# Attention, a mixture of experts and a dense layer on one core: where the guard's checks stand, and the order of two experts' first rows

## The chip, the cores and the metric

The kernel runs on one core of one Trainium2 chip. The metric is the device time of one launch in microseconds (us), the median of several runs. Each engine works through its own queue in order: PE (TensorE) multiplies matrices into PSUM, DVE (VectorE) and ACT (ScalarE) work element by element and also read PSUM, POOL (GpSimd) works on SBUF, and SP (SyncE) only issues DMAs. Engines wait for each other by semaphores.

## The reference, cut to what matters

Everything is float32. A recurrent attention with a decaying state per head is followed by a mixture of eight experts, of which each token takes one, and by a dense layer.

```python
B, H, S, D = 4, 8, 768, 40
for t in range(S):                       # attention: one state (D x D) per batch and head
    y[t] = r[t] @ state
    Sa = state @ a[t]
    state = state * w[t] - outer(Sa, b[t]) + outer(v[t], k[t])
x = y, heads side by side                # 3072 tokens x 320
e = argmax(x @ w_gate); g = softmax(x @ w_gate)[e]
x = g * (relu(x @ w1[e]) @ w2[e])        # 8 experts, 320 -> 1024 -> 320
h = x @ w_in                             # dense, 320 -> 2048 -> 320
out = (max(h, 0) + alpha * min(h, 0)) @ w_out
```

## The kernel before, in words

**Attention (class `Attention`).** The recurrence is solved in chunks of 64 steps. Four chunks of two batches make a group (`o`); there are six groups, and each needs per chunk and head the inverse of a triangular 64x64 matrix, called T here. `prepare` (L438) loads w, k, b and a and makes running products with two scans on DVE, s (L465) and q (L467); between them stand a reciprocal, and behind them a copy of the scan's first columns to `o.s0`, on ACT (L471). `products` (L477) multiplies on PE (lp) and lays the parts out, `sides` (L506) transposes. `inverse` (L526) solves the 32x32 diagonal blocks column by column on DVE (`ut`, L551 and L553), transposes the result twice on DVE (`ttc`, L573, and `t11`, L576), copies its four diagonal blocks of 32 partitions into T (`diagonal`, L565; L569), and then, for each half of the group, multiplies twice on PE (zp, yp) with copies on ACT behind each (z, L601; T, L610). The guard: `check` (L429) squares a tile on ACT and keeps the sum, so that values too large for this method can be told at the end; if one is found, or if an expert has too many or too few tokens, the flag is set and a slow general program runs after this one.

The state then goes through 48 slots (`run`, L734; a chunk of 64 steps, two batches at a time), each a chain PE, ACT, DVE, POOL, PE. The other groups' `prepare`, `products` and `inverse` are laid into the slots by `plan`. The first group has its T made before the first slot (`o.start`), in a region where DVE, POOL and ACT keep the order of the program. Everywhere else the framework's planner orders each engine's queue: by the order of the program, but an instruction that its time model takes to be ready can go ahead of one that isn't. `tc.issue_after(i)` keeps what is traced under it behind `i` on `i`'s engine.

**Routing (class `Router`).** `tiles` (L937) takes 128 tokens of two batches, finds each token's expert and its place there, and scatters the rows to `xs_d` in DRAM by an indirect DMA on POOL (L980); an expert has room for 448 rows (`CAP`). `under` (L986) tells whether expert 0 has at least 256 rows by then.

**Experts (class `Moe`, `run` L1158).** Weights and rows are split into a rounded part (hi, on ACT) and the rest (lo, on DVE or POOL), and three products stand for one. `prep_expert` (L1094) prepares an expert's weights in six pieces: raw load by SP into one of three buffers named `raw` (L1073, L1089), hi on ACT, lo on DVE. `group` (L1181) does an expert's rows in eight chunks: `hidden` (L1130) is the first layer of 128 hidden units on PE (ph), relu and split by ACT (hh, L1137) and DVE (hl, L1140); `layer2` (L1142) adds the chunk before to the sums (po). `between` (L1203) traces side work into the chunks: all six pieces of the next expert at chunk 1, behind the last load of rows (`self.x_dma`) and the last scatter; `decode` (L1043) of the dense weights, which lie in DRAM as 64-bit floats, whole, at expert 0; the dense weights' own preparation, lo on POOL, in experts 6 and 7.
Expert 0's first 256 rows (`early`, L1032) are loaded into a `raw` buffer two slots before attention ends and done first; its rows from 256 on are loaded when the last scatter has landed (L1104), then done, then expert 1 with 448 rows, and so on. Expert 7 does the first layer for 256 rows but the second for the first 128 only, writes those, then does the others, so that the dense layer's gather (L1125) can begin.

**Dense layer.** Six blocks of 512 tokens, gathered from `ys_d`, 16 chunks each.

Of the kernel before, what the change touches and what calls it, by code (L numbers as in the profile page):

```python
# [19 lines left out]
P = 128  # L20
B, H, S, D = 4, 8, 768, 40
N = B * S
DM = H * D
# [222 lines left out]
def gemm_k(nc, out, wt, c0, c1, xt, a, b):  # L246
# [9 lines left out]
    for i, (l, r) in enumerate(seq):  # L256
        mm(nc, out, l, r, i == 0, i == len(seq) - 1)
# [31 lines left out]
class Attention:  # L289
# [148 lines left out]
    def prepare(self, o, pg):  # L438
# [27 lines left out]
        nc.vector.reciprocal(self.d1q.rearrange("p (c t) -> p c t", t=CW)[:, :, 0], s3[:, :, 0])  # L466
        nc.vector.tensor_tensor_scan(qt.rearrange("p a c t -> p (a c t)"), wz[:, :nw], self.d1q, 0.0, ALU.mult, ALU.max)  # L467
# [3 lines left out]
        nc.scalar.copy(o.s0[:, p4, 2 * half:2 * half + 2], s3[:, :, 0].rearrange("p (a c) -> p a c", c=2))  # L471
# [54 lines left out]
    def inverse(self, o):  # L526
# [38 lines left out]
        def diagonal(half):  # L565
            for q in (1, 3, 0, 2):
                r = slice(32 * q, 32 * q + 32)
                eng = nc.vector if o.start and half == 0 else nc.gpsimd
                eng.tensor_scalar(o.tt[half][r, :, :, 32 * q:32 * q + 32], ttc[r, 2 * half:2 * half + 2], 1.0, 0.0, op0=ALU.mult, op1=ALU.add)  # L569
# [13 lines left out]
        for half in range(2):  # L583
            if half:
                vacant(1)
                diagonal(1)
                self.check(ut, ut, 0.01)
                self.check(l1.rearrange("p c u j -> p (c u) j"), ttc.rearrange("p c u t -> p (c u) t"), 0.01)
# [14 lines left out]
            if o.start:  # L603
                self.fill(yp, 8)
# [129 lines left out]
    def run(self, rt, sp, moe, ctx):  # L734
# [91 lines left out]
        at(n_slots - 2, 2, lambda: early(0))  # L826
# [70 lines left out]
class Router:  # L897
# [22 lines left out]
    def setup(self):  # L920
        nc, k = self.nc, self.k
        nc.gpsimd.affine_select(k.upper, k.ones, pattern=[[1, P]], compare_op=ALU.is_gt, fill=0.0, base=0, channel_multiplier=-1)
        iota_i = self.cp.tile([P, E], I32, name="iota_i")
# [13 lines left out]
    def tiles(self, sp, work, b0, t, yt):  # L937
# [48 lines left out]
        if (b0, t) == (B - 2, S // P - 2):  # L986
            nc.vector.tensor_scalar(self.under, self.run[:, :1], self.BASE + EARLY * P - 0.5, None, op0=ALU.is_lt)
# [27 lines left out]
class Moe:  # L1015
# [16 lines left out]
    def early(self, work):  # L1032

        xr = self.rp.tile([P, 1024], F32, name="raw")[:, :EARLY * DM].rearrange("p (t d) -> p t d", d=DM)
        self.nc.sync.dma_start(xr, self.rt.xs_d[:EARLY * P, :].rearrange("(t p) d -> p t d", p=P))
        yield
        self.xt0 = transpose_split(self.nc, self.k, self.ap, lambda n: work("tr_ps", [P, n], "w1"), xr, EARLY * P, "xt0", 1)
# [5 lines left out]
    def decode(self, src, name):  # L1043
# [17 lines left out]
        return out  # L1061

    def prep_in(self, wt, src, eng):

        nc = self.nc
        nf = src.shape[1]
# [314 lines left out]
```

## Time and profile before

| | us |
|---|---|
| median of 3 runs | 1084.41 (1084.05 to 1087.19) |
| profiled execution | 1090.49 |
| its span, first to last instruction | 1088.8 |
| mean granted PE clock over the span | 0.961 |

| engine | busy us | share |
|---|---|---|
| PE | 980.7 | 90% |
| DVE | 681.9 | 63% |
| ACT | 536.5 | 49% |
| POOL | 490.9 | 45% |

The profile is of one execution. All times in it are from the span's first instruction. Busy time of PE counts matmuls, whose ends are modelled; a matmul that runs at half the clock is busy twice as long. Attention lasts until about 475 us, the experts until about 728, the dense layer until the end.

### The profile page before, as it was taken

The page shows a single profiled execution, that of the slowest core. Times are in us where ns is not written, and L with a number is a line of the kernel's source. Part 1 is how long each engine was busy: PE and PEld are TensorE (multiplying, and loading weights), DVE is VectorE, ACT ScalarE, POOL GpSimd, SP SyncE. Part 2 cuts the span into 40 slices and gives each one's busy share as a digit, 9 for nine tenths or more (in the row PEclk, how much of TensorE's full clock was granted, in tenths as well). Part 3 has the DMA queues.
Part 4 walks back from the last instruction along what each step waited for, and adds up shares of the span by engine and source line. Part 5 has one row for each costly group of instructions (what it writes and reads, how often), then busy time and mean ns, then how long its engine had stood idle before and what let it go on. Part 6 is the DMA issues. An engine that isn't in the chain of part 4 may idle for free. (4 is left out here: it accounts for less than half of the span.)

```text
span 1088.8 us, 24353 instructions
## 1 busy us (share of the span) xinstructions
PE 980.7 (90%) x9213; PEld 871.9 (80%) x9213; DVE 681.9 (63%) x1493; ACT 536.5 (49%) x1303; POOL 490.9 (45%) x571
## 2 busy tenths in 40 slices
PE   2669987888879998887999999999999999999997
PEld 2557776777668777776899999899898988988986
DVE  9795968868978695556899753243444444344533
ACT  4657766686677777645677544421212222222211
POOL 7766677785867645320000003524435343534332
PEclk8669999999999999898999999999999999999999
DMA  4462323333323234427999643410000000000000
GB/s 121 103 204 72 93 73 81 90 77 83 89 77 84 55 68 105 111 55 262 324 332 321 212 149 106 124 46 7 19 25 25 25 25 25 26 25 25 25 1 28
DMA packets 128320, 103.33 MB, mean 95 GB/s; under 512 B 90564, under 2 KB 111044, under 8 KB 128196
## 3 DMA queue, kind: packets, MB, share of 16 engines
q1 hardware_dynamic: 125892, 93.83, 30.1%
q0 software_dynamic: 2304, 7.87, 2.3%
q8 instruction: 75, 1.23, 0.5%
q14 instruction: 49, 0.40, 0.1%
HBM read 79.39 MB, written 22.28 MB: 93 GB/s over the span
## 5 line engine op out<-in xcount | busy, mean ns | idle before, releaser
L234 POOL TENSOR_TENSOR gl<-g,gh 128x512 fp32r<-128x512 f32 x96 | 123.6, 1290 | 216.4 <-ACT gh L233 124.8
L233 ACT ACTIVATE gh<-g 128x512 fp32r<-128x512 f32 x96 | 60.8, 633 | 251.9 <-DVE g L1268 178.2
L1267 DVE TENSOR_SCALAR g<-ph,al 128x512 f32<-128x512 f32 x96 | 72.1, 751 | 160.1 <-POOL gl L234 77.6
L243 PE MATMUL ph<-x2thi,win 128*128 128x512 f32 x480 | 159.5, 397 | 0.0
L243 PE MATMUL po<-wout,gh 128*128 128x320 f32 x768 | 139.0, 310 | 0.0
L243 PEld LDWEIGHTS po<-wout,gh 128*128 128x128 f32 x768 | 122.0, 188 | 5.6
L243 PE MATMUL ph<-x2tlo,win 128*128 128x512 f32 x288 | 114.3, 397 | 0.0
L243 PEld LDWEIGHTS ph<-x2thi,win 128*128 128x128 f32 x480 | 88.6, 188 | 14.9
L243 PE MATMUL po<-we,hh 128*128 128x320 f32 (+1 forms) x480 | 92.5, 322 | 6.8 <-ACT hh L1137 6.1
L243 PE MATMUL ph<-xthi,we 128*128 128x448 f32 (+2 forms) x360 | 97.5, 342 | 0.1
L1076 POOL TENSOR_TENSOR win<-raw,win 128x1024 fp32r<-128x1024 f32 x4 | 9.6, 2406 | 185.3 <-ACT win L1074 185.2
L243 PEld LDWEIGHTS po<-we,hh 128*128 128x128 f32 (+1 forms) x480 | 75.9, 187 | 10.7 <-ACT hh L1137 6.7
L243 PE MATMUL po<-wout,gl 128*128 128x320 f32 x384 | 82.9, 312 | 0.0
L243 PE MATMUL ph<-xtlo,we 128*128 128x448 f32 (+2 forms) x216 | 73.7, 342 | 0.9 <-DVE xtlo L276 0.9
L494 PE MATMUL lp<-kb,abd 128*128 128x128 f32 x352 | 58.2, 309 | 17.2 <-POOL abd L474 10.3
L474 POOL TENSOR_TENSOR abd<-ra,q 40x512 f32<-40x512 f32 x44 | 61.4, 1396 | 22.4 <-DVE q L467 12.3
L243 PEld LDWEIGHTS ph<-xthi,we 128*128 128x128 f32 x360 | 66.5, 195 | 3.3 <-ACT xthi L273 0.2
L1268 DVE SCALAR_TENSOR_TENSOR g<-ph,g 128x512 f32<-128x512 f32 x96 | 66.3, 691 | 3.1
L243 PEld LDWEIGHTS po<-wout,gl 128*128 128x128 f32 x384 | 64.0, 188 | 3.0
L494 PEld LDWEIGHTS lp<-kb,abd 128*128 128x128 f32 x352 | 49.1, 212 | 21.6 <-POOL abd L474 10.8
L553 DVE TENSOR_TENSOR ut<-ut,tmp 128x31 f32<-128x31 f32 (+15 forms) x186 | 62.5, 336 | 3.6
L689 PE MATMUL sa<-vg,pw 128*64 128x104 f32 x768 | 57.2, 262 | 6.8 <-issue 4.6
(217 smaller groups left out, 2241.5 us busy)
## 6 DMA issues: line engine op xcount, KB each, us to landing
raw<-in_moe_w_dram SPq DMA_DIRECT2D x16, 512.0 KB
raw<-in_moe_w_dram SPq DMA_DIRECT2D x16, 480.0 KB
kb<-in_kbP_dram SPq DMA_DIRECT2D x44, 160.0 KB
r<-in_moe_w_in_dram SPq DMA_DIRECT2D x10, 512.0 KB
r<-in_moe_w_out_dram SPq DMA_DIRECT2D x10, 512.0 KB
xs_d<-tt SPq DMA_DIRECT2D x8, 560.0 KB
raw<-in_moe_w_dram SPq DMA_DIRECT2D x16, 256.0 KB
wz<-in_wP_dram SPq DMA_DIRECT2D x48, 81.4 KB
```

What stands on the lines that cost most here:

```text
L233: nc.scalar.activation(hi, src, AF.Copy)
L234: return lo_eng.tensor_tensor(lo, src, f32(hi), op=ALU.subtract)
L243: return nc.tensor.matmul(out, lhsT=lhsT, rhs=rhs, start=start, stop=stop)
L474: nc.gpsimd.tensor_tensor(abd[r, :, q * C:(q + 1) * C], ra[r], qc[r, :, :C], op=ALU.mult)
L494: nc.tensor.matmul(lp[:, i], lhsT=abd[:, i, c2, :], rhs=kb[:, i, c2, :], start=True, stop=True)
L553: nc.vector.tensor_tensor(ut[:, j + 1:, :m], ut[:, j + 1:, :m], tv, op=ALU.subtract)
L689: nc.tensor.matmul(sa[q * 64:q * 64 + 64, i], lhsT=x.pw[:, i, q * C:(q + 1) * C], rhs=x.vg[:, i, q, :], start=True, stop=True)
L1076: eng.tensor_tensor(wt[:, 3 + c, cs], raw, f32(wt[:, c, cs]), op=ALU.subtract)
L1267: nc.vector.tensor_scalar(g, ph, 0.0, al[:, f:f + 1], op0=ALU.min, op1=ALU.mult)
L1268: nc.vector.scalar_tensor_tensor(g, ph, 0.0, g, op0=ALU.max, op1=ALU.add)
```

## The change

The chunks of experts 0 and 1 change order: expert 0's first 256 rows, expert 1's first 256 rows, expert 0's other 192, expert 1's other 192. For that, `early` loads 256 rows of both experts into two `raw` buffers, two slots earlier than before, and `under` looks at both counts one tile earlier. `prep_expert`, `decode` and the dense preparation are traced one piece per chunk, each behind that chunk's hh and hl on ACT and DVE; expert 1's pieces in expert 0's early group, expert 2's in expert 1's early group, `decode` from the third group on. The `issue_after` of the last scatter and of the last load of rows goes. The dense preparation's lo alternates between DVE and POOL, and most of it moves from expert 6 to expert 7. In expert 7 the second tile's sums are ordered behind the last first-layer matmul (`ph_i`) in place of the last sum (`last`).
In attention, `o.s0`'s copy moves from ACT to DVE, between the reciprocal and the second scan; in the first group two of the four diagonal copies (blocks 1 and 3) move from DVE to ACT; the checks of `ut` and of `l1` move from between the halves to behind the copies of T of the first and the second half; the eight filler matmuls before yp go. `iota_i` takes the memory of `slot`.

```diff
+        nc.vector.tensor_copy(o.s0[:, p4, 2 * half:2 * half + 2], s3[:, :, 0].rearrange("p (a c) -> p a c", c=2))
         nc.vector.tensor_tensor_scan(qt..., wz[:, :nw], self.d1q, 0.0, ALU.mult, ALU.max)
...
-        nc.scalar.copy(o.s0[:, p4, 2 * half:2 * half + 2], s3[:, :, 0].rearrange("p (a c) -> p a c", c=2))
...
             for q in (1, 3, 0, 2):
+                if o.start and half == 0 and q % 2:
+                    nc.scalar.copy(to, src)
+                else:
+                    eng = nc.vector if o.start and half == 0 else nc.gpsimd
...
-                self.check(ut, ut, 0.01)
-                self.check(l1..., ttc..., 0.01)
...
-            if o.start:
-                self.fill(yp, 8)
...
-                    nc.scalar.activation(tt[lo, c2, :, hi], out(yp, c2, q), AF.Copy, scale=-1.0)
+                    done = nc.scalar.activation(tt[lo, c2, :, hi], out(yp, c2, q), AF.Copy, scale=-1.0)
+            with self.tc.issue_after(done.ins):
+                src = l1.rearrange("p c u j -> p (c u) j") if half else ut
+                self.check(src, src, 0.01)
...
-        at(n_slots - 2, 2, lambda: early(0))
+        at(n_slots - 4, 2, lambda: early(0))
...
-        xr = self.rp.tile([P, 1024], F32, name="raw")...
-        self.nc.sync.dma_start(xr, self.rt.xs_d[:EARLY * P, :]...)
+        rows = []
+        for e in range(2):
+            xr = self.rp.tile([P, 1024], F32, name="raw")...
+            self.nc.sync.dma_start(xr, self.rt.xs_d[e * CAP:e * CAP + EARLY * P, :]...)
+            rows.append(xr)
...
-                if e == E - 2 and f >= 4:
-                    for _ in range(2):
+                if e == E - 1 or e == E - 2 and f in (5, 7):
+                    with tc.issue_after(self.hh_i.ins), tc.issue_after(self.hl_i.ins):
                         next(prep, None)
...
-                if f == 1 and e + 1 < E:
-                    with tc.issue_after(self.rt.last.ins), tc.issue_after(self.x_dma.ins):
-                        whole(self.prep_expert(e + 1, nc.vector))
+                if f == 0 and 1 < e < E - 1:
+                    coming.append(self.prep_expert(e + 1, nc.vector))
+                if f and 1 < e < E - 1:
+                    with tc.issue_after(self.hh_i.ins), tc.issue_after(self.hl_i.ins):
+                        next(coming[-1], None)
...
-                if (e, f) == (0, 0):
+                if f in ((1, 4, 7), (1, 4, 7), (0, 2, 4, 6), (0, 2, 4, 6), (0, 2, 4, 6), (0, 4), (), ())[e]:
                     with tc.issue_after(self.hh_i.ins), tc.issue_after(self.hl_i.ins):
-                        w_in, w_out = self.decode(self.w_in, "w_in"), self.decode(self.w_out, "w_out")
+                        w_in, w_out = next(decoded)
...
             if e == 0:
+                second, third = self.prep_expert(1, nc.vector), self.prep_expert(2, nc.vector)
+                rest = self.load_x(0, EARLY)
+                def ahead(f):
+                    if f > 1:
+                        with tc.issue_after(self.hh_i.ins), tc.issue_after(self.hl_i.ins):
+                            next(second, None)
+                    if f == 4:
+                        xt1.append(after(lambda: transpose_split(..., self.early_rows, EARLY * P, "xt1")))
+                def behind(f):      # the same with third; at f == 5: xt1.append(after(rest))
...
+                group(self.xt0, 0, EARLY, 0, ehs, between=ahead)
+                group(xt1[0], 0, EARLY, 0, ehs, between=behind, wts=self.wts[1], po=po1)
+                group(xt1[1], EARLY, 4, 0, ring, between=between)
+            elif e == 1:
                 group(xt, EARLY, 4, 0, ring, between=between)
             elif e == E - 1:
...
-                with tc.issue_after(self.last.ins):
+                with tc.issue_after(self.ph_i.ins):
                     for f in range(NF1):
                         self.layer2(po, *hs[f], w2s, f, NF1, True, (1,))
-                    group(xt, 2, 4, 2 * P, ring)
+                    group(xt, 2, 4, 2 * P, ring, between=lambda f: f % 2 and next(prep, None))
+                    whole(prep)
```

## Rows read from the trace of the kernel before

**Rows 1.** The page's slices of the span, 40 equal ones: PE's busy tenths.
```profile
PE   2669987888879998887999999999999999999997
```

**Rows 2.** Busy time by stretch: engines' busy us (instructions), granted clock, DMA share, GB/s.
```profile
core 0: us, PE busy (x) PEld busy (x) DVE busy (x) ACT busy (x) POOL busy (x), PEclk, DMA share, GB/s
470.00:477.50 7.50, 4.46 (x53) 3.86 (x53) 3.65 (x9) 2.09 (x7) 1.64 (x2) 1.00 0.43 90
494.30:524.20 29.90, 22.10 (x124) 19.48 (x123) 21.63 (x42) 18.71 (x37) 0.00 (x0) 0.81 0.81 257
703.50:712.10 8.60, 5.91 (x28) 5.57 (x28) 0.42 (x1) 2.06 (x4) 6.37 (x5) 0.80 0.17 53
```

**Rows 3.** Timeline of PE, chunks of experts 0, 1, 2: start us, us, instruction.
```profile
477.49 0.39 PE L243 MATMUL ph<-xt0hi,we 128*128 128x256 f32 x1
...
485.36 0.28 PE L243 MATMUL ph<-xt0hi,we 128*128 128x256 f32 x1
...
487.20 0.28 PE L243 MATMUL ph<-xt0hi,we 128*128 128x256 f32 x1
...
518.18 0.25 PE L243 MATMUL ph<-xthi,we 128*128 128x192 f32 x1
...
519.81 0.25 PE L243 MATMUL ph<-xthi,we 128*128 128x192 f32 x1
...
552.16 0.37 PE L243 MATMUL ph<-xthi,we 128*128 128x448 f32 x1
...
576.60 0.37 PE L243 MATMUL ph<-xthi,we 128*128 128x448 f32 x1
...
579.82 0.36 PE L243 MATMUL ph<-xthi,we 128*128 128x448 f32 x1
```

**Rows 4.** Timeline, all engines, expert 0: hl, loads, a weight piece; brackets: idle before.
```profile
485.15 0.42 DVE L1140 SCALAR_TENSOR_TENSOR ehl<-ph,ehh 128x256 fp32r<-128x256 f32 x1 [0.81 <-ACT ehh L1137]
...
486.89 0.87 SPq L1104 DMA_DIRECT2D xe<-xs_d  x2
...
488.94 2.10 SPq L1073 DMA_DIRECT2D raw<-in_moe_w_dram  x4
...
494.61 1.06 ACT L1074 ACTIVATE we<-raw 128x1024 fp32r<-128x1024 f32 x1 [1.51 <-DMA raw<-in_moe_w_dram]
...
495.70 1.22 DVE L1076 TENSOR_TENSOR we<-raw,we 128x1024 fp32r<-128x1024 f32 x1 [2.15 <-ACT we L1074]
```

**Rows 5.** Timeline, all engines, attention's start.
```profile
71.20 1.95 DVE L573 STREAM_TRANSPOSE ttc<-ut 128x1024 f32<-128x1024 f32 x1
...
77.25 1.97 PE L597 MATMUL zp<-tt,l 128*64 128x64 f32 x32 [7.29 <-DVE tt L569]
...
80.71 0.20 ACT L471 COPY s<-s 104x8 f32<-104x8 f32 x1 [4.69 <-DVE s L465]
...
82.71 1.06 ACT L434 ACTIVATE ttc<-l 128x1024 f32<-128x1024 f32 x1 [0.37 <-POOL tt L569]
...
86.63 1.24 DVE L467 TENSOR_TENSOR_SCAN q<-wz,d1q 104x520 f32<-104x520 f32 x1
...
87.31 1.09 PE L649 MATMUL pp<-tt,la 128*64 128x128 f32 x16 [1.13 <-ACT tt L610]
...
90.95 2.44 POOL L474 TENSOR_TENSOR abd<-ra,q 40x512 f32<-40x512 f32 x2
```

**Rows 6.** Line 471, the first-column copy: ns min/median/max; then what its engine waited for.
```profile
L471 ACT COPY s<-s x24: 187/203/228, 6.4 to 321.4; 104x8 f32<-104x8 f32 x24
...
  DVE s L465: 36.8, 18
```

**Rows 7.** Timeline, all engines, expert 7.
```profile
705.04 1.00 ACT L1090 ACTIVATE wout<-raw 128x960 fp32r<-128x960 f32 x1 [2.28 <-DMA raw<-w_out]
...
706.37 0.56 PE L243 MATMUL po<-we,hh 128*128 128x320 f32 x2 [2.69 <-ACT hh L1137]
```

**Rows 8.** Line 470, DVE: ns min/median/max. Page: POOL's pieces, busy us, mean ns.
```profile
L470 DVE TENSOR_TENSOR kb<-kb,s x4: 659/696/1667, 7.3 to 13.3; 104x512 f32<-104x512 f32 x4
...
L1076 POOL TENSOR_TENSOR win<-raw,win 128x1024 fp32r<-128x1024 f32 x4 | 9.6, 2406 | 185.3 <-ACT win L1074 185.2
```

More of the change, by code (lines that the diff above doesn't have):

```diff
@@ L256, in gemm_k @@
     for i, (l, r) in enumerate(seq):
-        mm(nc, out, l, r, i == 0, i == len(seq) - 1)
+        last = mm(nc, out, l, r, i == 0, i == len(seq) - 1)
+    return last
 def transpose_split(nc, k, sp, psum, rows, n, nm, bufs=2):
@@ L1167, in run @@
         pa = ctx.enter_context(tc.tile_pool(name="fm_pa", bufs=1, space=PSUM, reuse_waits="tile"))
-        sums = lambda: [p.tile([P, DM], F32, name=f"po{t}") for t, p in enumerate((pa, pa, pb, pb))]
+        bank = lambda t: (pa, pa, pb, pb)[t].tile([P, DM], F32, name=f"po{t}")
+        sums = lambda: [bank(t) for t in range(4)]
         r6 = ExitStack()
@@ L1172, in run, with both, group @@
         self.n_small = 0
-        load = self.load_x(0, EARLY)
+        def both():
+            for a in self.decode(self.w_in, "w_in"):
+                yield a, None
+            for b in self.decode(self.w_out, "w_out"):
+                yield a, b
+        decoded = both()
+        coming = []
         nxt = win = prep = w_in = w_out = None
+        ehs = lambda f: [self.ap.tile([P, EARLY * P], F32R, name=n, bufs=2) for n in ("ehh", "ehl")]
+        ye1 = self.ap.tile([P, EARLY, DM], F32, name="ye1")
         for e in range(E):
             w1s, w2s = self.wts[e]
-            po = sums()
+            po = [bank(t) for t in range(EARLY)] if e == 0 else [None] * EARLY + [bank(t) for t in range(EARLY, 4)] if e == 1 else sums()
             ye = sp.tile([P, 4, DM], F32, name="ye", tag="orow", bufs=1)
             ys = self.rt.ys_d[e * CAP:(e + 1) * CAP, :]
-            def group(xt, t0, t1, x0, tiles, ts=None, between=None):
+            def group(xt, t0, t1, x0, tiles, ts=None, between=None, wts=(w1s, w2s), po=po):
+                w1s, w2s = wts
                 ts = ts or range(t0, t1)
@@ L1226, in run, with after @@
             ring = lambda f: [sp.tile([P, 4 * P], F32R, name=n, tag=n) for n in ("hh", "hl")]
+            def after(fn):
+                with tc.issue_after(self.last.ins):
+                    return fn()
             if e == 0:
-                group(self.xt0, 0, EARLY, 0, lambda f: [self.ap.tile([P, EARLY * P], F32R, name=n, bufs=2) for n in ("ehh", "ehl")])
-                xt = load()
+                second, third = self.prep_expert(1, nc.vector), self.prep_expert(2, nc.vector)
+                rest = self.load_x(0, EARLY)
+                xt1 = []
+                def ahead(f):
[3 more added lines that the diff above has]
+                    if f == 4:
+                        xt1.append(after(lambda: transpose_split(nc, k, sp, self.psum_t, self.early_rows, EARLY * P, "xt1")))
+                def behind(f):
+                    if f > 1:
+                        with tc.issue_after(self.hh_i.ins), tc.issue_after(self.hl_i.ins):
+                            next(third, None)
+                    if f == 5:
+                        xt1.append(after(rest))
+                group(self.xt0, 0, EARLY, 0, ehs, between=ahead)
+                whole(second)
+                for t in range(EARLY):
+                    to_sbuf(t)
+                po1 = [bank(t) for t in range(EARLY)]
+                group(xt1[0], 0, EARLY, 0, ehs, between=behind, wts=self.wts[1], po=po1)
+                whole(third)
+                for t in range(EARLY):
+                    to_sbuf(t, ye1, po1)
+                nc.sync.dma_start(self.rt.ys_d[CAP:CAP + EARLY * P, :].rearrange("(t p) d -> p t d", p=P), ye1)
+                po[EARLY:] = [bank(t) for t in range(EARLY, 4)]
+                group(xt1[1], EARLY, 4, 0, ring, between=between)
+            elif e == 1:
@@ L1230, in run @@
                 group(xt, EARLY, 4, 0, ring, between=between)
             elif e == E - 1:
-                hs = [[hp.tile([P, 2 * P], F32R, name=f"{n}{f}") for n in ("hh", "hl")] for f in range(NF1)]
+                hs = [ehs(f) if f < 2 else [hp.tile([P, 2 * P], F32R, name=f"{n}{f}") for n in ("hh", "hl")] for f in range(NF1)]
                 group(xt, 0, 2, 0, lambda f: hs[f], (0,), between)
```

49 lines of the change are left out of this document (26 added, 23 removed).

## The prediction, made before the change was run

> **What bounds the kernel now.** I read the page's row of 40 slices first: TensorE (PE) is busy for nine tenths or more of nearly every slice from the twentieth on, and below that before it [rows 1]. So most experts and the dense stage can't be shortened by a change that leaves PE its work; what can be won is where PE stands idle or is granted less than its full clock. The busy times by stretch give three of those places: attention's tail (470.0 to 477.5: 4.46 of 7.50 us busy), expert 0's second half and the change to expert 1 (494.3 to 524.2: 22.10 of 29.90 us busy, mean granted clock 0.81), and expert 7 (703.5 to 712.1: 5.91 of 8.60 us, clock 0.80) [rows 2]. The fourth is attention's start. Then I read the timeline at each, for what ends the waits.
>
> **Experts 0 and 1, the largest term.** Expert 0's first matmul starts at 477.49, expert 2's at 552.16: 74.67 us [rows 3]. A chunk (first layer of one block of 128 hidden units, second layer of the one before) takes 1.84 us with 256 rows (485.36 to 487.20), 1.63 us with 192 (518.18 to 519.81) and 3.22 us with 448 (576.60 to 579.82), where nothing is late. Expert 2 as a whole takes 27.66 us (552.16 to 579.82), so 8 x 3.22 leaves 1.9 us for the transposes of 448 rows [rows 3].
> Why it is slow now: the rest of expert 0's rows is loaded only after the last scatter (issue at 486.89), and expert 1's weights are tied behind that load: their DMAs leave SP at 488.94, the first piece is on ACT at 494.61 and on DVE at 495.70 [rows 4]. All six pieces, and the decoding of the dense weights, then sit on ACT and DVE among the small copies of each chunk, with 257 GB/s on DMA [rows 2].
> What the change makes of it: expert 0's 256 rows, expert 1's 256, expert 0's 192, expert 1's 192. The tie to the last load goes, the pieces come one per chunk, and the decoding only after both early groups. PE's work is then 2 x 8 x 1.84 + 2 x 8 x 1.63 = 55.5 us, plus transposes of 256, 192, 192 and 448 rows, 1088/448 x 1.9 = 4.6 us: 60.1 us. That expert 1 is now split is paid in it (1.84 + 1.63 - 3.22 = 0.25 us a chunk). At best this gives 74.7 - 60.1 = 14.6 us.
> I take off 4 us. Per chunk of 1.84 us DVE has 0.42 + 1.22 = 1.64 us and ACT 1.06 for the piece and about 0.4 for hh [rows 4]: it fits, but the piece stands ahead of the next chunk's copies, and DVE has the transposes' low parts and the copies of the sums besides (some 2 us a group). Raw buffers are the other limit. There are three, the early rows hold two of them, and one turn is 494.61 - 488.94 = 5.7 us of loading plus 1.06 + 1.22, 8 us with DMA crowded [rows 4]. Expert 1's first-layer pieces are wanted only when its group begins, 15 us after expert 0's, so two to three buffers with a piece loaded ahead just do. I take **-10.5 us**; ends -14.6 and -3.5 (rival 1).
>
> **Attention's tail.** The early rows are now read two slots earlier, so they no longer wait for the scatter of the last tile but one. PE is idle for 3.0 us in 470.0 to 477.5 [rows 2]; the early transposes and first matmuls can stand there, though not in all of it, since the last slots' own chain stays: **-2.5 us**; ends -3.0 and 0. The two loads go into SP's queue in front of the last slots' loads. I cost that at nothing, because the scatter that they wait for is two tiles back; if it isn't done, the last slots' loads stand behind it and these 2.5 us are gone.
>
> **Attention's start.** The transpose to ttc ends at 71.20 + 1.95 = 73.15, and PE's zp starts at 77.25, after 7.29 us idle until DVE's diagonal copies, which stand behind a second transpose [rows 5]. Blocks 1 and 3, which zp reads, now go to ACT. The price of such a copy (32x512) on ACT is not shown: it lies between the 0.2 us of the 104x8 copy [rows 6] and the 1.06 us of the 128x1024 check [rows 5]; 0.6 for half the columns. Then zp starts at about 74.5: 2.7 us. The z copies stood behind the first-column copy, which ACT started at 80.71 after 4.69 us idle for DVE's scan, while zp was through at 77.25 + 1.97 = 79.22 [rows 5]: 1.5 us, gone with that copy's move. Then the T copies stood behind the check of ttc (1.06 us at 82.71) [rows 5]. So pp, at 87.31, comes some 5 us earlier.
> That is not what reaches the end. The second group's products stood behind the same chain on POOL: its abd started at 90.95, and its q is ready at 86.63 + 1.24 = 87.87 [rows 5], so 3 of the 5 us carry on. Against it, DVE gets the first-column copy, ahead of the scan that POOL waits for: 24 copies of 0.2 us by ACT's row [rows 6] (0.1 to 0.4 on DVE), eight of them before this point, 1.6 us. The eight filler matmuls that go stand where PE waits anyway. Net **-1.5 us**; ends -5 and +2.
>
> **Attention's slots.** ACT was held 36.8 us in 18 waits by the scan before that copy [rows 6]. Little of it comes back, as PE's work per slot stays: the checks behind the T copies at five group boundaries give perhaps 0.5 us each, ACT's freedom as much again, and DVE's 16 further copies take up to 3.2. **-2 us**; ends -6 and +3. The guard's one more DVE instruction on the counts, and the tile that now shares memory, I cost at nothing: neither is on a chain.
>
> **Expert 7.** Now the last chunk's hh stands behind a weight piece for which ACT waited 2.28 us (705.04), so PE waits 2.69 us before 706.37 [rows 7], and the 8.6 us around it run at 0.80 clock [rows 2], 1.7 us. Ordering the second tile's sums behind the last first-layer matmul, not the last sum, lets PE fill that wait: -4.4 us. But expert 7 gets ten pieces in place of six, eight of them in chunks of 11 matmuls (some 1.4 us, estimated from 14 in 1.84), and the raw buffers turn out a piece every 8 / 3 = 2.7 us: five chunks late by 1.3 us, +6.5. Some of it the planner orders away. **-1.5 us**; ends -4.4 and +6.5.
> A price that speaks against alternating DVE and POOL: DVE's product of two SBUF tiles took 659 ns at least and 1667 ns at most in one form [rows 8], so 1.0 us may be lost beside POOL; five such pieces make 5 us, on a DVE with slack. The Trainium skill (SBUF — State Buffer, "Who interferes with whom") says that such a DVE instruction contends with a GpSimd one that reads SBUF, and that the loser blocks for the other's whole length. The two ends of the row look like that; with POOL's 2.4 us a piece [rows 8] the rule would make it up to 12 us, and if DVE had no slack the forecast would be up to 12 us later.
>
> **Sum.** -10.5 - 2.5 - 1.5 - 2 - 1.5 = -18 us. The profiled execution took 1090.49 us, its span and 1.7 around it, so 1072.5; it was 6.1 us above the median of 1084.41, and I forecast **1066 us** for the median (1084.4 - 18).
>
> **Rivals.**
> 1. Weights still late: the planner leaves the load of expert 0's rest (waiting until 486.89) ahead of expert 1's loads in SP's queue. Its pieces then arrive as now, and expert 1's early group starts near 501.5, not 493, and ends 16 us later; then 1.5 + 13 + 1.5 + 16 us: expert 2 at 549.5, 3 us won instead of 10.5. For it: that load comes first in the program. Against: the planner moves ready loads forward. 1084.4 - 10.5 = 1074.
> 2. Everything fits: 14.6 + 3 + 5 + 6 + 1.4 = 30: 1054. For it: DVE and ACT have the room on paper. Against: the shared raw buffers.
> 3. Slower: one piece per chunk turns ACT into a gate. It works in order, and a piece whose raw load hasn't landed holds back the next hh, as at 705.04 [rows 7]. With two to three buffers and 8 us a turn a piece comes every 2.7 to 4 us, say 3.3, against chunks of 1.84 and 1.4: 12 early chunks late by 1.5 us and five of expert 7 by 1.9 are 27 us, and at the 0.81 clock of such stretches [rows 2] some 25 us of matmuls cost 5 us more: 32 against gains of 14.6 + 2.5 + 3.5 + 4.4 = 25, so +7, 1091. It decides once a piece takes more than about 2.9 us. Against: with DMA uncrowded a load should take less than 5.7 us, and the decoding that crowds it is moved away.
> 4. The change does nothing: attention's sides cancel, the weights are late as in rival 1 and expert 7 loses 3 us: 1082 to 1086.
>
> **Chances.** Forecast 0.52 (1059 to 1070), rival 1 0.20 (1070 to 1079), rival 2 0.13 (1050 to 1059), rival 3 0.10, rival 4 0.05. A measurement of this kernel tells a change from none at about 0.3%, 3.3 us. Faster by more: 0.52 + 0.20 + 0.13 = 0.85; within: 0.05; slower: 0.10. The range leaves out rival 3, rival 4 and the lower part of rival 2: 1053 to 1081.
>
> **What would show it.** Right: expert 1's first matmul of 256 rows within 17 us of expert 0's, no PE wait over 1 us until expert 2, which starts 62 to 66 us after expert 0; PE under 2 us idle in the 7.5 us before; pp's first matmul near 83; no wait of 2.7 us in expert 7. Wrong: expert 1's loads issued after those of expert 0's rest (rival 1); ACT idle for raw loads with PE waiting for the hh behind them (rival 3); a DVE that makes POOL later by more than 1.6 us before 70 us.

## The result and the profile after

The changed kernel takes 1093.24 us (median of 6 runs, 1092.22 to 1097.99), the kernel before 1085.70 on the same chip (6 runs, 1082.55 to 1089.43): ratio 1.0087, 95% interval 1.0065 to 1.0110. It is slower; the forecast was 1066. The profiled execution took 1093.25 us, span 1091.5, mean granted clock 0.957.

The page of the changed kernel: busy us, share and instructions of each engine, then PE's busy tenths in 40 slices, to hold against [rows 1].
```profile
PE 981.6 (90%) x9261; PEld 873.0 (80%) x9261; DVE 695.5 (64%) x1534; ACT 537.2 (49%) x1293; POOL 481.2 (44%) x565
...
PE   2569888889889988888999999989999999999997
```
PE has as much work as before, so what counts is again where it waits. Timeline of PE in the changed kernel, the starts that answer to [rows 3]: expert 0, expert 1's early group, expert 2, expert 3.
```profile
479.78 0.39 PE L244 MATMUL ph<-xt0hi,we 128*128 128x256 f32 x1
...
500.69 0.41 PE L244 MATMUL ph<-xt1hi,we 128*128 128x256 f32 x1
...
550.05 0.37 PE L244 MATMUL ph<-xthi,we 128*128 128x448 f32 x1
...
577.18 0.37 PE L244 MATMUL ph<-xthi,we 128*128 128x448 f32 x1
```
Expert 1's early group comes 20.9 us after expert 0's (the forecast's mark was 17), and expert 2 70.3 us after expert 0, in place of 74.7 [rows 3]: some 4 of the 10.5 us are there. Busy time by stretch, columns as in [rows 2]: the last slots, the end of expert 0's early group, the start of the dense layer. PE is busy there for 18.63 of 25 us, 5.79 of 10 and 5.88 of 6.5.
```profile
455.00:480.00 25.00, 18.63 (x270) 15.62 (x265) 13.56 (x40) 15.22 (x36) 7.68 (x13) 0.86 0.54 148
491.00:501.00 10.00, 5.79 (x40) 5.32 (x39) 3.48 (x9) 3.62 (x7) 0.00 (x0) 0.96 0.78 248
724.50:731.00 6.50, 5.88 (x31) 4.48 (x30) 4.28 (x9) 3.29 (x7) 0.00 (x0) 1.00 0.20 63
```
Attention's start, timeline, to hold against [rows 5]: the solve's end, the two copies that moved to ACT, zp, pp (the first product with T), and the first slot's sa.
```profile
74.18 1.94 DVE L579 STREAM_TRANSPOSE ttc<-ut 128x1024 f32<-128x1024 f32 x1
...
76.21 1.25 ACT L572 COPY tt<-ttc 32x512 f32<-32x512 f32 x2
...
77.51 1.97 PE L601 MATMUL zp<-tt,l 128*64 128x64 f32 x32 [4.56 <-ACT tt L572]
...
90.12 0.32 PE L654 MATMUL pp<-tt,la 128*64 128x128 f32 x1
...
95.39 0.30 PE L694 MATMUL sa<-vg,pw 128*64 128x104 f32 x1
```
The copies on ACT take 0.6 us each, as estimated, and zp's wait shrinks from 7.29 to 4.56 us. But the solve itself ends 3.0 us later (74.18, before 71.20), so pp is 2.8 us late instead of some 5 early. Why stands in the first-column copy's own rows: its durations (ns min/median/max), then the timeline of DVE and POOL around the longest.
```profile
L469 DVE COPY s<-s x24: 119/276/2441, 6.2 to 320.1; 104x8 f32<-104x8 f32 x24
```
```profile
39.34 2.44 DVE L469 COPY s<-s 104x8 f32<-104x8 f32 x1
39.44 2.34 DVE L553 TENSOR_TENSOR tmp<-ul,ut 128x31 f32<-128x31 f32 x1
...
38.98 0.43 POOL L378 MEMSET sm<- 104x416 f32 x1
39.37 0.98 POOL L378 MEMSET pw<- 128x512 f32 x2
40.30 1.45 POOL L378 MEMSET yt<- 128x512 f32 x3
41.80 0.29 POOL L927 TENSOR_SCALAR_AFFINE_SELECT upper<-ones 128x128 bf16<-128x128 bf16 x1
```
A copy of 8 columns stood for 2.44 us, from 39.34 to 41.78, while POOL ran six memsets back to back to 41.75, and the first step of the solve (L553) stood behind it. On ACT the same copy never took over 228 ns [rows 6]. Of the 24, 13 took over 0.25 us, and each of these ended 25 to 35 ns behind the end of an instruction of POOL; the other 11 took 119 to 160 ns. The first eight, which the prediction priced at 1.6 us, took 4.9 us together, all 24 took 10.6.

Stages of all kernels, in us, from the first matmuls of the stages in their traces (one profiled execution each; "s" is the copy on DVE as a copy; the last column is the timed ratio to the kernel before):

| kernel | slot 0 at | slots 0-40 | slot 40 to expert 0 | experts 0, 1 | 2 to 6 | expert 7 + first dense block | ratio |
|---|---|---|---|---|---|---|---|
| before | 90.7 | 334.7 | 52.1 | 74.7 | 138.9 | 91.3 | 1 |
| changed (s) | 95.4 | 331.6 | 52.8 | 70.3 | 139.1 | 96.2 | 1.0087 |
| 1 attention alone (s) | 97.0 | 334.1 | 50.9 | 75.2 | 139.7 | 89.2 | 1.0036 |
| 2 experts alone | 91.9 | 334.4 | 48.6 | 69.9 | 139.1 | 95.0 | 0.9992 |
| 3 copy on ACT | 91.5 | 330.1 | 51.9 | 69.8 | 139.1 | 95.2 | 1.0007 |
| 4 early rows later (s) | 95.8 | 338.3 | 50.1 | 68.9 | 139.1 | 93.3 | 1.0055 |
| 5 copy as reduction | 91.0 | 333.5 | 50.5 | 70.0 | 139.1 | 96.0 | 1.0005 |
| 6 rows of their own | 91.5 | 331.5 | 53.2 | 69.8 | 139.1 | 95.6 | 0.9966 |
| 7 + rest later | 90.7 | 330.5 | 50.8 | 70.1 | 139.1 | 96.0 | 0.9959 |
| 8 dense preparation back | 91.8 | 335.8 | 53.4 | 70.4 | 140.4 | 94.1 | 0.9985 |
| 9 order of sums back | 91.1 | 330.7 | 51.6 | 70.7 | 139.1 | 93.9 | 0.9987 |
| 10 both back | 91.3 | 329.5 | 52.2 | 71.6 | 139.7 | 95.2 | 1.0019 |
| 11 loads tied | 92.8 | 328.2 | 53.0 | 64.4 | 139.1 | 95.2 | 0.9961 |
| 12 5 + 10 + 11 | 92.0 | 330.9 | 51.0 | 64.5 | 140.2 | 95.4 | 0.9994 |
| 13 copy alone (s) | 96.5 | 339.4 | 56.0 | 70.5 | 138.6 | 88.4 | 1.0080 |
| 14 attention, reduction | 91.9 | 338.7 | 51.5 | 72.2 | 138.5 | 88.9 | 1.0013 |
| 15 whole pieces | 91.6 | 333.6 | 51.4 | 74.5 | 144.5 | 88.3 | 1.0048 |
| 16 11 + 15 | 92.1 | 335.0 | 50.7 | 69.0 | 143.7 | 90.4 | 0.9964 |
| 17 11 + two in expert 6 | 92.4 | 331.2 | 53.3 | 64.6 | 139.1 | 91.0 | 0.9888 |
| 18 11 + order of sums | 92.5 | 333.7 | 47.7 | 64.5 | 139.1 | 93.7 | 0.9879 |

The slots differ by up to 10 us between executions of kernels with the same slots, so less is not read from one there. The ratios' intervals are about +-0.002 to +-0.003 (17 and 18 +-0.004). The kernel before was timed anew beside 1 to 4, 5 to 8, 9 to 12, 13 to 16, and 17 and 18; its medians there lie between 1085.28 and 1091.53 us, so small differences between ratios of different sets are not read either.

### The profile page after: what moved, and what is told of

Read it like the earlier page. It is cut to its first block, busy times and chain, and to the rows that moved or that the text cites. A ratio compares the mean times of both kernels' runs of the same rounds, so it can differ in the third digit from the quotient of the medians.

```text
span 1091.5 us, 24464 instructions
## 1 busy us (share of the span) xinstructions
PE 981.6 (90%) x9261; PEld 873.0 (80%) x9261; DVE 695.5 (64%) x1534; ACT 537.2 (49%) x1293; POOL 481.2 (44%) x565
## 4 chain that ended last, share of the span: by engine, by line
PE 59%; DVE 12%; DMA 5%; issue 4%; ACT 3%; POOL 3%; SPq 0%; POOLq 0%; DVEq 0%; ACTq 0%
PE ph L244 25%; PE po L244 23%; PE tr_ps L272 2%; DMA raw<-in_moe_w_dram 2%; DVE tmp L553 2%; PE pp L654 2%; DVE va L699 1%; DVE ut L555 1%; PE sa L694 1%; PE rvp L665 1%; DVE q L470 1%; DVE s L467 1%; PE yc L710 1%; DMA xs_d<-xr,sli 1%; PE xp L244 1%
## 5 line engine op out<-in xcount | busy, mean ns | idle before, releaser
L244 PEld LDWEIGHTS ph<-x2thi,win 128*128 128x128 f32 x480 | 89.2, 189 | 17.2 <-DVE g L1326 2.3
L1088 POOL TENSOR_TENSOR win<-raw,win 128x1024 fp32r<-128x1024 f32 x2 | 4.8, 2400 | 202.5 <-ACT win L1085 202.5
L244 PE MATMUL ph<-xthi,we 128*128 128x448 f32 (+2 forms) x360 | 90.6, 326 | 0.0
L244 PE MATMUL po<-we,hh 128*128 128x320 f32 (+1 forms) x440 | 82.6, 313 | 3.5 <-ACT hh L1150 2.9
L244 PEld LDWEIGHTS po<-we,hh 128*128 128x128 f32 (+1 forms) x440 | 67.9, 180 | 6.7 <-ACT hh L1150 3.7
L244 PE MATMUL ph<-xtlo,we 128*128 128x448 f32 (+2 forms) x216 | 69.9, 325 | 0.0
L1150 ACT ACTIVATE hh<-ph 128x448 fp32r<-128x448 f32 (+2 forms) x70 | 31.7, 455 | 74.1 <-PE ph L244 54.3
L496 PEld LDWEIGHTS lp<-kb,abd 128*128 128x128 f32 x352 | 50.8, 219 | 20.9 <-POOL abd L476 10.8
L244 PEld LDWEIGHTS ph<-xthi,we 128*128 128x128 f32 x360 | 63.0, 189 | 2.8
```

The costliest lines, as they stand in the source:

```text
L244: return nc.tensor.matmul(out, lhsT=lhsT, rhs=rhs, start=start, stop=stop)
L496: nc.tensor.matmul(lp[:, i], lhsT=abd[:, i, c2, :], rhs=kb[:, i, c2, :], start=True, stop=True)
L1150: self.hh_i = nc.scalar.activation(hh[:, :n], ph[:, :n], AF.Relu)
```

## Experiments

Theory A: the copy on DVE is shut out by POOL (start and slots), and two early loads in the ring of three raw buffers make weights late. The rivals, and the theories B to D that came later, stand in the expectations.

**1 and 2. Each half of the change alone.** The diff of 1 is the hunks in `prepare` and `inverse`, that of 2 all others.


> Attention's edits alone (the first-column copy on DVE, the diagonal copies on ACT, the checks behind the copies of T, no filler matmuls); the experts as before. Theory A (the copy on DVE is held by POOL: one of 2.4 us in the first group puts the solve 3 us later, and the slots give back little of it): 1 to 4 us slower than before. Rival (attention's edits gain the 3.5 us of the prediction and the whole loss is in the experts): 2 to 5 us faster than before.

> The experts' edits alone, attention's prepare and inverse as before (the early rows are read two slots earlier, as in the changed kernel). Theory A (two early loads hold two of the three raw buffers, expert 0's own pieces of weights slide into the last slots and hold ACT there: +6 us at the last slots; -4.4 us in experts 0 and 1; +5 us in expert 7 and the first dense block): 4 to 8 us slower than before, and expert 0's third piece on ACT still behind a wait of 3 to 4 us for its raw load. Rival (the loss is attention's): 2 to 6 us faster than before.


1: 1.0036 (1.0013 to 1.0059), slower, as theory A. 2: 0.9992 (0.9971 to 1.0012), no difference, missed by both: the experts' edits cost nothing in all. Expert 0's pieces do slide into the last slots (in the changed kernel the third is on ACT at 463.58 after 3.83 us of waiting for its load, before at 439.02), but the slots that they leave are shorter by nearly as much: slots 40 to 45 take 32.2 us in the changed kernel, 36.0 before.

**3. The changed kernel, copy back on ACT.**
```diff
-        nc.vector.tensor_copy(o.s0[...], s3[:, :, 0]...)      # ahead of the scan q
+        nc.scalar.copy(o.s0[...], s3[:, :, 0]...)             # behind it, as before
```


> The changed kernel with the first-column copy back on ACT, where it was. Theory A: the solve ends near 71 us again instead of 74, and the time falls by 2 to 4 us against the changed kernel, to 1089 to 1091. Rival (the checks' and diagonal copies' new places are what delays the start, or the slots take the 3 us up): within 1 us of the changed kernel, 1093.


1.0007 (0.9989 to 1.0026); the solve ends at 71.0. Without the copy on DVE the loss is gone, which is more than expected; but the gain that was forecast isn't there either.

**4. Early rows read two slots before the end.** `at(n_slots - 4, ...)` to `at(n_slots - 2, ...)`.


> The changed kernel with the early rows read two slots before the end of attention, as before, so behind expert 0's six pieces of weights in the ring of raw buffers. Theory A: expert 0's pieces are done by 450 us again, ACT has no wait of over 1 us for them in the last five slots, slot 45 to 47 takes 8 to 9 us instead of 16, and the time falls by 3 to 6 us against the changed kernel, to 1087 to 1090. Rival (the last slots are slow by the early transposes or the routing on PE and DVE, not by the ring): within 1.5 us of the changed kernel.


1.0055 (1.0033 to 1.0077), 0.3% below the changed kernel's ratio, the intervals overlapping. The last slots are short again (slot 45 to expert 0: 16.2 us, changed 20.6), but from slot 40 on only 2.7 us are won. Inconclusive in size.

**5. The same place on DVE, as a reduction.**
```diff
-        nc.vector.tensor_copy(o.s0[...], s3[:, :, 0].rearrange("p (a c) -> p a c", c=2))
+        nc.vector.tensor_reduce(o.s0[...], s3[:, :, :1].rearrange("p (a c) t -> p a c t", c=2), axis=AX.X, op=ALU.max)
```


> The changed kernel with the first-column copy at the same place on DVE, written as a reduction over an axis of length one in place of a copy. Theory A (a DVE copy from SBUF to SBUF is shut out while POOL executes, a reduction isn't): none of the 24 takes over 0.35 us, the solve ends near 71.5 us instead of 74, and the time falls by 4 to 7 us against the changed kernel, to 1086 to 1089. Rival (the instruction's place ahead of the scan costs, or POOL shuts out any DVE instruction there): some of the 24 still take 0.5 to 2.5 us and end with an instruction of POOL, and the time stays at 1091 to 1094.


1.0005 (0.9979 to 1.0031). The line's durations, then DVE and POOL at the place of the 2.44 us above:
```profile
L469 DVE TENSOR_REDUCE s<-s x24: 112/119/158, 5.8 to 314.5; 104x8 f32<-104x8 f32 x24
```
```profile
38.45 0.13 DVE L469 TENSOR_REDUCE s<-s 104x8 f32<-104x8 f32 x1
38.56 0.19 DVE L553 TENSOR_TENSOR tmp<-ul,ut 128x31 f32<-128x31 f32 x1
...
38.09 0.44 POOL L378 MEMSET sm<- 104x416 f32 x1
38.47 0.99 POOL L378 MEMSET pw<- 128x512 f32 x2
```
The same bytes at the same place, beside the same memsets, in 0.13 us, and the solve goes on at once. So it is the form of the instruction, and neither its place nor DVE's load. The Trainium skill (SBUF — State Buffer, "Who interferes with whom") says just that: a DVE copy can take the port pair that DVE shares with GpSimd, the loser of which blocks wholly, and a reduction never does. By its words one instruction blocks the other; here the copy was out over six.

**13. The copy alone, on the kernel before.** The diff is the first one of the change.


> The kernel before with one edit of the change alone: the first-column copy on DVE, between the reciprocal and the second scan. Theory A (DVE is shut out while POOL executes): pp's first matmul 3 to 5 us later than the 87.3 of before, and 4 to 7 us slower, ratio 1.003 to 1.007. Rival (the copy costs only together with the other edits of attention): within 2 us of before, ratio 0.998 to 1.002.


1.0080 (1.0049 to 1.0111), pp at 92.0. One line costs nearly as much as the whole change, and more than theory A expected.

**14. Attention's edits with the reduction.**


> Experiment 1's kernel (attention's edits alone, ratio 1.0036) with the copy as a reduction. Theory A: attention's other edits then show what they are worth, pp 1 to 3 us earlier than in the kernel before, ratio 0.996 to 0.999. Rival (the diagonal copies on ACT, the missing filler matmuls or the checks' new place cost as well): ratio 1.001 to 1.004.


1.0013 (0.9984 to 1.0042): the other edits are worth nothing that can be measured, where theory A expected 0.996 to 0.999. pp comes at 86.7, slot 0 at 91.9; without the copy on DVE pp comes 0.1 to 2.7 us earlier than the 87.3 of before in all kernels with the new attention, but slot 0 is at 90.7 to 92.8 whether with the old attention (90.7, 91.9) or the new. PE isn't waiting in between: in 14 it works from pp at 86.66 to slot 0 at 91.92 without a gap, and the 32 matmuls of the second half's yp and eight of lp, which in the kernel before come behind slot 0's first sa, now stand ahead of it.

Against experiment 1 (1.0036), 14 puts the copy at only 0.2%, with intervals that overlap; 3, 5 and 13 put it at 0.8%. That it costs is shown, the size is known to lie between.

**6 and 7. The raw ring and SP's queue.** In the changed kernel, SP, ACT and PE at the end of expert 0's early group:
```profile
488.58 0.49 SPq L1084 DMA_DIRECT2D raw<-in_moe_w_dram  x1
492.40 0.85 SPq L1117 DMA_DIRECT2D xe<-xs_d  x2
493.30 0.59 SPq L1084 DMA_DIRECT2D raw<-in_moe_w_dram  x1
...
497.29 1.06 ACT L1085 ACTIVATE we<-raw 128x1024 fp32r<-128x1024 f32 x1 [5.71 <-DMA raw<-in_moe_w_dram]
...
498.67 0.85 PE L244 MATMUL po<-we,ehh 128*128 128x320 f32 x4 [3.63 <-ACT ehh L1150]
```
Half of a piece is loaded at 488.58; the other half stands in SP's queue behind xe, the load of expert 0's other rows, which waits 3.3 us for the last scatter, and ACT behind the piece, with the next ehh behind ACT. Experiment 6 (on 3) gives the early rows other memory, 7 moves xe behind expert 1's pieces in the program:
```diff
-            xr = self.rp.tile([P, 1024], F32, name="raw")[...]
+            xr = self.ye1 = self.ap.tile(...) if e else own.tile([P, EARLY, DM], F32, name="xe0")
...
-                rest = self.load_x(0, EARLY)                  # 7: called in behind(0)
```


> Experiment 3's kernel (first-column copy on ACT), and the two early loads of rows go to memory of their own instead of two of the three raw buffers. Theory A (the ring): expert 0's six pieces are on ACT without a wait of over 1.5 us, slot 40 to expert 0's first matmul takes 47 to 49 us instead of 52, experts 0 and 1 together 65 to 68 instead of 70, and the time is 4 to 8 us below experiment 3's 1086.8: 1079 to 1083. Rival (the load of expert 0's rest, waiting for the last scatter in SP's queue ahead of half a piece, alone sets experts 0 and 1, and the last slots are slow by PE's early transposes): experts 0 and 1 stay at 69 to 70, and the time is 0 to 2 us below.

> As experiment 6, and the load of expert 0's other rows is traced behind expert 1's pieces, at the first chunk of expert 1's early group, and not at the start of expert 0's. Theory A (both, ring and SP's queue): expert 1's first 256-row matmul 15 to 17.5 us after expert 0's instead of 21, experts 0 and 1 together 62 to 65 us, and 2 to 5 us below experiment 6: 1075 to 1080. Rival (that load costs nothing once the ring is free): within 1.5 us of experiment 6.


6: 0.9966 (0.9944 to 0.9989); 7: 0.9959 (0.9936 to 0.9982). Expert 1's early group now starts after 16.6 us, as theory A of 7 said, but experts 0 and 1 still take 70: the stall went from the third piece to the fifth. Experiment 7, the same engines:
```profile
485.87 0.86 SPq L1122 DMA_DIRECT2D xe<-xs_d  x2
...
487.48 0.38 SPq L1107 DMA_DIRECT2D raw<-in_moe_w_dram  x1
...
492.88 1.00 ACT L1108 ACTIVATE we<-raw 128x960 fp32r<-128x960 f32 x1 [5.49 <-DMA raw<-in_moe_w_dram]
...
494.21 1.44 PE L244 MATMUL po<-we,ehh 128*128 128x320 f32 x4 [4.54 <-ACT ehh L1155]
```
The planner had moved xe ahead of the fifth piece again, and xe stood in SP's queue for 4.1 us until the last scatter had landed. Both expectations missed on experts 0 and 1.

**11. Experiment 7 with ties on SP.**
```diff
+                        with tc.issue_after(self.raw_i.ins):   # expert 1's last raw load
                             rest.append(self.load_x(0, EARLY))
+ ... the first decode loads likewise, behind expert 2's last raw load
```


> Experiment 7's kernel (early rows in memory of their own, ratio 0.9959) with two ties on SP: the load of expert 0's other rows behind the load of expert 1's last piece, and the first loads for decoding behind the load of expert 2's last piece. Theory C (in experiment 7 that load still went ahead in SP's queue, waited there for the last scatter and held back expert 1's fifth piece, 5.5 us of waiting on ACT and 4.5 on PE): no wait of PE over 2 us until expert 2, experts 0 and 1 together 64 to 66 us instead of 70, ratio 0.990 to 0.993. Rival (ACT's wait is the loads' own time, 4 to 5 us each when two share the queues): a wait of 3 us or more again, 68 to 70 us, ratio 0.995 to 0.997.


PE's waits from expert 0 to expert 2, all of them (us, times, longest), and the stretch's busy time:
```profile
PE po L244 <- DVE sl L977: 0.6, 1, 0.6
PE po L244 <- ACT hh L1155: 0.3, 1, 0.3
PE ph L244 <- ACT xt1hi L275: 0.2, 1, 0.2
```
```profile
474.00:539.00 65.00, 63.75 (x478) 59.83 (x474) 45.27 (x118) 36.74 (x83) 2.99 (x2) 1.00 0.66 206
```
Experts 0 and 1 take 64.4 us, as theory C said; the ratio, 0.9961 (0.9939 to 0.9983), isn't as low as its forecast and is that of 7, from another set: the 5.7 us of the stage don't show in it. 11 ties two loads at once, xe and the decoding's, so the share of each isn't known, and the ties without memory of their own for the early rows weren't tried.

**8, 9 and 10. Expert 7.** On experiment 3: the dense preparation as before (8), `ph_i` back to `last` (9), both (10).
```diff
-                with tc.issue_after(self.ph_i.ins):
+                with tc.issue_after(self.last.ins):           # 9, 10
...
-                if e == E - 1 or e == E - 2 and f in (5, 7):  # 8, 10: two pieces a chunk from f = 4 of expert 6
```


> Experiment 3's kernel with the dense weights' preparation as before the change: four chunks of expert 6 with two pieces each, the rest in expert 7 one per chunk, all low parts on POOL. Theory A (the ten pieces in expert 7 on DVE, POOL and ACT cost): expert 7 to the dense layer takes 33 to 35 us instead of 37, the first dense block 56.6 instead of 58 to 59.6, and the time is 2 to 5 us below experiment 3's 1086.8: 1082 to 1085. Rival (the loss there is from the order of the second tile's sums, not from the preparation): within 1.5 us of experiment 3.

> Experiment 3's kernel (ratio to before 1.0007) with one edit undone: in expert 7 the second tile's sums stand behind the last sum again, and not behind the last first-layer matmul. Theory B (pulling those sums ahead leaves PE nothing to do while the dense layer's first rows are transposed and its first g is made: 1.9 us idle and some us at the lower clock): from expert 7's first matmul to the dense layer's second block takes 91 to 93 us instead of 95.3, and the ratio falls to 0.996 to 0.998. Rival (the ten pieces in expert 7 are what costs): 95 us again, and the ratio stays at 1.000 to 1.002.

> Experiment 8's kernel (dense preparation as before, ratio 0.9985) with the second tile's sums behind the last sum as well, so all of expert 7 as before the change. Theory B: expert 7 to the dense layer's second block as before, 91.3 us (experiment 8: 94.1), ratio 0.995 to 0.997. Rival (that stretch is longer because the decoding now ends later, or the second block's gather): 93 us or more, ratio 0.998 to 1.000.


0.9985 (0.9960 to 1.0010), 0.9987 (0.9967 to 1.0007), 1.0019 (0.9999 to 1.0039). 8 and 9 lie below experiment 3's 1.0007, but within the intervals, and 10, with both, doesn't: its stage took 95.2 us, where theory B said 91.3, and theory B fell. ACT in the kernel before: expert 7's own last pieces, 40 us before expert 7 begins (691.03), then the first pieces of the dense weights.
```profile
649.17 1.63 ACT L1090 ACTIVATE we<-raw 128x960 fp32r<-128x960 f32 x2 [1.19 <-DMA raw<-in_moe_w_dram]
...
669.20 2.97 ACT L1074 ACTIVATE win<-raw 128x1024 fp32r<-128x1024 f32 x3
```
ACT in the changed kernel: expert 7's own last piece, 4 us before expert 7 begins (689.15), then pieces of the dense weights, whose loads waited on SP for up to 4.3 us for the low part that frees their raw buffer; below, PE's longest wait in expert 7 and the one at the dense layer's start.
```profile
685.17 0.73 ACT L1103 ACTIVATE we<-raw 128x640 fp32r<-128x640 f32 x1
...
697.16 1.06 ACT L1085 ACTIVATE win<-raw 128x1024 fp32r<-128x1024 f32 x1 [2.72 <-DMA raw<-w_in]
...
701.68 1.06 ACT L1085 ACTIVATE win<-raw 128x1024 fp32r<-128x1024 f32 x1 [2.92 <-DMA raw<-w_in]
...
708.91 1.01 ACT L1103 ACTIVATE wout<-raw 128x960 fp32r<-128x960 f32 x1 [3.46 <-DMA raw<-w_out]
...
698.54 0.56 PE L244 MATMUL po<-we,hh 128*128 128x320 f32 x2 [1.39 <-ACT hh L1150]
...
732.25 0.72 PE L244 MATMUL ph<-x2thi,win 128*128 128x512 f32 x1 [1.87 <-DVE g L1326]
```
**15 and 16. Six pieces at one chunk again** (on 10, and on 11).
```diff
-                if f == 0 and 1 < e < E - 1:                  # one piece per chunk
+                if f == 1 and 1 < e < E - 1:
+                    whole(self.prep_expert(e + 1, nc.vector))
```


> Experiment 10's kernel (all of expert 7 as before the change, ratio 1.0019) with the six pieces of the experts 3 to 7 traced at one chunk again, as before the change, and not one per chunk. Theory D (one per chunk makes expert 7's own pieces end only when expert 6 does, they hold the raw buffers, and the dense preparation is pushed into expert 7): expert 7's last piece is on ACT before the middle of expert 6, from expert 7's first matmul to the dense layer's second block 91 to 92.5 us instead of 95.2, ratio 0.997 to 0.999. Rival (the later decoding makes the dense preparation late): 94 us or more, ratio 1.000 to 1.002.

> Experiment 11's kernel (ratio 0.9961) with expert 7 as in experiment 15. Theory D: experts 0 and 1 take 64 to 65 us and expert 7 to the second dense block 91 to 92.5, 4 us below experiment 11: ratio 0.990 to 0.993, 1075 to 1078 us by a kernel before of 1086. Rival (given back): 0.995 to 0.998.


Theory D was right about expert 7 (15: 88.3 us with the first dense block, against 95.2 in 10, which differs by the pieces alone), but experts 2 to 6 take 144.5 instead of 139.7, and the ratio is 1.0048 (1.0023 to 1.0073). 16: 0.9964 (0.9939 to 0.9990), no better than 11: experts 0 and 1 take 69.0 us, where 64 to 65 were expected. They run as in 11 until their last 17 us; there three pieces in a row stand on ACT ahead of the next hh, and another piece waits for its load, with PE behind:
```profile
529.49 2.95 ACT L1090 ACTIVATE we<-raw 128x1024 fp32r<-128x1024 f32 x3
...
532.71 0.71 PE L244 MATMUL po<-we,hh 128*128 128x320 f32 x3 [1.17 <-ACT hh L1155]
...
536.87 1.00 ACT L1108 ACTIVATE we<-raw 128x960 fp32r<-128x960 f32 x1 [2.82 <-DMA raw<-in_moe_w_dram]
```
Pieces that nothing ties to a chunk are thus drawn into the experts before. What they meet in experts 2 to 6 (the decoding is there now) wasn't taken apart.

**12, 17 and 18. Combinations.** 12 is 5, 10 and 11 in one. 17 is 11 with 10, and expert 7's own pieces two per chunk; 18 is 11 with 9.
```diff
                     with tc.issue_after(self.hh_i.ins), tc.issue_after(self.hl_i.ins):
-                        next(coming[-1], None)
+                        for _ in range(2 if e == E - 2 else 1):    # 17
+                            next(coming[-1], None)
```


> Experiments 5, 10 and 11 in one: first-column copy on DVE as a reduction, early rows in memory of their own, the two ties on SP, expert 7 and the dense preparation as before the change. If the three causes are apart from each other: 0.4 per cent below experiment 11 by expert 7, so a ratio of 0.986 to 0.990, 1071 to 1076 us where the kernel before takes 1086. If what one gives back is taken by the next wait: 0.993 to 0.997.

> Experiment 11's kernel with the dense preparation and the order of expert 7's second tile as before the change, and expert 7's own six pieces two per chunk in the first three chunks after expert 6's first; the other experts keep one piece per chunk. Theory D: experts 2 to 6 take 139 to 140 us, expert 7 to the second dense block 89 to 92 instead of 95.2, ratio 0.990 to 0.994. Rival (two pieces in a chunk hold hh as whole pieces did): experts 2 to 6 at 142 us or more, ratio 0.995 to 0.998.

> Experiment 11's kernel with the second tile's sums of expert 7 behind the last sum again, nothing else. From experiment 9: the first dense block 56.5 us instead of 58.0, so a ratio 0.1 to 0.2 per cent below experiment 11's 0.9961: 0.993 to 0.996. Rival: what the order gives in the dense block is paid in expert 7, as in part in experiment 9: the same ratio as experiment 11.


12: 0.9994 (0.9971 to 1.0017), above both of its expectations: expert 7's stage stays at 95.4 us. 17: 0.9888 (0.9846 to 0.9931), 1077.39 us. 18: 0.9879 (0.9836 to 0.9922), 1078.43. Both beat both kernels, and both are lower than expected. In 17 expert 7's last own piece, and PE's two longest waits from there to the second dense block:
```profile
667.80 0.74 ACT L1108 ACTIVATE we<-raw 128x640 fp32r<-128x640 f32 x1 [0.44 <-DMA raw<-in_moe_w_dram]
```
```profile
PE po L244 <- ACT hh L1155: 1.3, 2, 1.0
PE ph L244 <- DVE ehl L1158: 1.0, 1, 1.0
```
Its stages are as theory D said (139.1 and 91.0). By stages 18 differs from 11 by 1.5 us in the dense layer, yet by ratio by 0.8%: the kernel before, timed beside each, took 1085.28 us beside 11 and 1089.42 beside 17 and 18. How much these two win is known only by their intervals, 0.7 to 1.6%.

## Why the prediction was wrong

The forecast was -18 us; measured are +9 (0.87% of 1085.7). Three terms failed, each by some 6 to 8 us: the first-column copy, experts 0 and 1, and expert 7. The copy made the change a loss; without it (experiments 3 and 5) the change gives nothing, so the forecast of a gain failed by the other two. By the stages, with means over kernels that share the stage:

- **The first-column copy, priced at "0.1 to 0.4 on DVE", 1.6 us for the start.** The first step that failed is this cost: the eight copies took 4.9 us, one of them 2.44. Slot 0 comes at 96.2 with the copy on DVE (four kernels), at 90.7 to 92.8 without: +4.4 to +4.9. The slots take 335.9 with it, 332.6 without (16 kernels): +3.3, within what one execution varies. Alone it costs 0.8% (13), or 0.2% between 1 and 14. I bounded a DVE copy by an ACT copy's row; the row that came nearer was [rows 8], one form on DVE between 659 and 1667 ns. I had read it, with the Trainium skill's rule beside it, and applied both to expert 7 only, where the price was small: there one DVE piece took 2.35 us beside POOL instead of 1.16.
- **Attention's other edits, -1.5 and -2.** The mechanisms are there (copies of 0.6 us on ACT, zp earlier), and pp gains up to 2.7 us, but slot 0 does not: PE now has the second half's yp and lp to do ahead of it. Experiment 14 measures no gain.
- **The tail, -2.5.** Slot 40 to expert 0 takes 51.6 us (eight kernels with the ring as changed) against 52.6 (four with the old experts): about -1, within the range. I costed the two loads at nothing in SP's queue. They took raw buffers that expert 0's own pieces needed and moved these into the last slots; but with rows of their own the stretch takes 51.4 us (seven kernels), so no price of it is shown here.
- **Experts 0 and 1, -10.5.** Measured -3.2 (70.0 against 73.2, four kernels each; 8 to 10, with the same edits here, took 70.4 to 71.6). The step that failed is the wait: one load in SP's queue. The sum of 64.1 was met once the loads were tied, 64.4 in experiment 11, but in part by luck: PE is busy for 63.2 of them and waits for 1.2, so the work was 3 us more than the 60.1 (transposes 5.8 for 4.6, and 1.3 of attention's last routing, which I left out), and the allowance of 4 for late pieces was too much. What kept it at 70 was rival 1's mechanism, xe in SP's queue waiting for the last scatter, with the ring or the decoding's loads beside it (their shares are open, see 11); I gave it 0.20 and a place before expert 1's first piece, and it struck in the third. 1.5 us of the baseline were the profiled execution's own (74.7; 75.2, 70.5 and 72.2 in others with these experts).
- **Expert 7, -1.5 (ends -4.4 and +6.5).** Measured +6.2 with the first dense block (95.6 against 89.4). I counted ten pieces in expert 7 at the raw buffers' rate, which the waits on SP bear out, and then trusted the planner to order part of it away. The step that failed is what I did not follow upstream: one piece per chunk makes expert 7's own pieces end with expert 6 (685.17; expert 7 starts at 689.15), and the dense pieces start behind them. 15 and 17 show it. The 1.87 us at the dense layer's start are not explained: they are gone in 9 and 15 to 18, but not in 10 and 12, which share the order of 9.

Sum: 4.9 + 3.3 - 1.1 - 3.2 + 6.2 = +10.1, against +9 measured; with the slots' 3.3 no surer than said, the agreement proves little. Of the rivals, the third came nearest in time (1091) and holds in part: ACT was a gate, but in single waits of 3 to 6 us behind single loads, not in every chunk.

## What to carry to other kernels

Price a moved instruction by a row of the engine that it goes to, next to the neighbour that it will have there; a small DVE copy between SBUF tiles is not small beside a busy POOL, and a reduction over an axis of one did the same work unhindered. When work is spread out, follow the shared buffers to the next user: who gets them later, and which in-order engine stands waiting with other work behind it. And take the base of a large term from more than one profiled execution.

## What the hardware showed that was not expected

- The copy on DVE (104 x 8) was shut out not for one instruction of POOL but for six in a row, 2.44 us; the six were memsets, which read nothing.
- The same bytes as a reduction took 112 to 158 ns in all 24 cases of experiment 5, and 111 to 163 in the 24 of experiment 14.
- A raw load of expert 1 took 5.4 us from its issue (487.48) to ACT's start on it (492.88) in experiment 7, with DMA 97% busy at 321 GB/s (487.5 to 492.9), while the same pieces were waited for by at most 1.2 us when xe and the decoding's loads came behind them (experiment 11).
